# A gated feed-forward kernel behind inducing-point attention: gate and value products issued back to back, a pipelined prologue, and early output weights

## The chip, the cores and the metric

The kernel runs on one core of a Trainium2 chip. The metric is the device time of one execution in microseconds. The engines are named PE (TensorE, matmul; PEld is its weight load), DVE (VectorE), ACT (ScalarE), POOL (GpSimd) and SP (SyncE, which issues most of the DMAs). A run more than 1.5% above the fastest of the same kernel is marked slow; ratios are of fast runs alone.

## The reference, cut to what matters

Two stages run over 4 batches of 12416 tokens of 128 features: attention through 32 inducing points, then a gated feed-forward layer of width 1536 with a gated residual.

```python
h = mab(inducing, x)                 # softmax over all tokens of the batch, 32 x 128
attn = mab(x, h)                     # each token: softmax over the 32 rows of h
g   = attn @ w_gate ; val = attn @ w_val          # 128 -> 1536
ffn = (gelu(g) * val) @ w_out                     # 1536 -> 128
out = attn + sigmoid(attn @ w_res) * ffn
```

Since attn is a mix of 32 rows of h, the kernel multiplies h by the weights once per batch (the "first layers" hg, hv, hr). Each token then needs only its 32 softmax weights (rt, transposed, in four copies) against those small matrices.

## The kernel before

Tokens go in groups of 512 (100 groups, 25 per batch, of which the last is a quarter). A full group has six slots. A slot makes two chunks of 128 hidden features: a gate pair and a value pair of matmuls (two row halves of 64 side by side), a gelu on ACT and a multiply on DVE. The output products of the group before are spread between them.

```python
    def gate_slot(gi, si):
        gv_t[gi, si] = wide_bank()           # one of three double banks of PSUM
        slot_mms(gi, si, hg_t)               # gate pair into the bank
        act.activation(ge, gv_t[gi, si], AC.Gelu, ...)
    def value_mms(gi, si):
        slot_mms(gi, si, hv_t)               # value pair into the SAME bank, so after the gelu
    def value_mul(gi, si):
        ve.tensor_tensor(u, ge, gv_t.pop((gi, si)), AL.mult)
    ...
            gate_slot(*nxt)                          # the gate pair of the next slot
            if prev and p == nper - 1:
                prev.mms(len(prev.todo)); ...; prev.end()   # DVE final multiply, POOL add, store
            if prev: prev.mms(quota // 2)            # 5 output products of the group before
            value_mms(gi, p); value_mul(gi, p)
            if prev: prev.mms(quota - quota // 2)    # 5 more
            if prev and p == 0:   prev.gate()        # 4 mixing products (32 rows), ACT tanh
            elif prev and p == 2: prev.residual()    # 4 mixing products (64 rows), ACT copy
            for f in todo.pop((g, p), []): f()       # pieces of the next batch's attention
```

The prologue handles the first batch's attention tile by tile: load x, split it on DVE and POOL into a high and a low fp16 half, transpose on PE, evict on ACT, score on PE, exponential on ACT, accumulate on PE. Ahead of the loop it makes all softmax weights of tiles 0 to 7, and only then loads and scales the output weights:

```python
    for j0 in range(PRE, 8 * PRE, 4 * PRE):
        ...
        for k in range(j0 // PRE, j1 // PRE):
            weights_b(0, k)                          # POOL multiply, DMA transpose by SP
    for o in range(0, FCH, PRE):
        sy.dma_start(wf, moe_w_out ...)              # SP's queue: behind the transposes
        ve.tensor_scalar(wO[...], wf, 0.5, None, op0=AL.mult)   # DVE's queue: ahead of the multiplies
```

The softmax here doesn't subtract the row's maximum and nothing guards it: scores larger than these inputs give would overflow.

Of the kernel before, what the change touches and what calls it, by code (L numbers as in the profile page):

```python
# [9 lines left out]
FP32 = mybir.dt.float32  # L10
# [4 lines left out]
AL = mybir.AluOpType  # L15
# [3 lines left out]
def kernel(  # L19
# [24 lines left out]
    M = inducing.shape[0]  # L44
    F = moe_w_gate.shape[1]
# [34 lines left out]
    def misc_bank():  # L80
        return ps_m.tile([P, TOK], FP32, name="ms", tag="ms")
# [7 lines left out]
    def blocks_of(k):  # L89
        return k * PRE, min(PRE, nblk - k * PRE)  # L90
# [110 lines left out]
    def res_layer(b):  # L201
        bank = misc_bank()
        pe.matmul(bank[:, :P], ht_t[b], wR, start=True, stop=True)
        hr = p_h.tile([P, P], FP16, name="hr", tag="hr")
        hr_t[b] = hr
        act.activation(hr, bank[:, :P], AC.Copy, bias=0.0, scale=1.0)

    def exp_b(b, j0, j1):
        n = (j1 - j0) * M
# [69 lines left out]
    def value_mms(gi, si):  # L279
        slot_mms(gi, si, hv_t)  # L280
# [7 lines left out]
    class Last:  # L288
# [17 lines left out]
                pe.matmul(self.ffn[:, k, :], u_t[self.gi, si][:, o:o + P], wO[:, fc, :],  # L306
                          start=(fc == 0), stop=(fc == FCH - 1))

        def mix(self, h, r):
            bank = misc_bank()  # L310
            for k in range(self.nk):
                pe.matmul(bank[:, k * P:(k + 1) * P],  # L312
                          rt_t[self.b, self.k][r, self.j0 + k, :],
                          h[r, :], start=True, stop=True)
            return bank

        def gate(self):
            bank = self.mix(hr_t[self.b], slice(0, M))
            self.th = p_fin.tile([P, TOK], FP32, name="th", tag="th")
            act.activation(self.th[:, :self.tw], bank[:, :self.tw], AC.Tanh,  # L320
                           bias=0.0, scale=0.5)

        def residual(self):
            bank = self.mix(ha_t[self.b], slice(0, 2 * M))
            self.at = p_fin.tile([P, TOK], FP32, name="at", tag="at")
            act.activation(self.at[:, :self.tw], bank[:, :self.tw], AC.Copy,  # L326
                           bias=0.0, scale=1.0)
# [42 lines left out]
    pieces = []  # L370
    for dst, src in ((wG, moe_w_gate), (wV, moe_w_val), (wR, moe_w_res)):
        n = dst.shape[1]
        for o in range(0, n, PRE * P):
            w = min(PRE * P, n - o)
            pieces.append((dst[:, o:o + w], src[:, o:o + w], w))

    def weight_in(i):
        dst, src, w = pieces[i]
        wf = p_x.tile([P, PRE, P], FP32, name="xf", tag="xf")
        xf_t["w", i] = wf  # L380
        sy.dma_start(wf.rearrange("p k c -> p (k c)")[:, :w], src)

    def weight_cast(i, eng):
        dst, src, w = pieces[i]
        eng.tensor_copy(dst, xf_t.pop(("w", i)).rearrange("p k c -> p (k c)")[:, :w])


    for k in range(ntile):
        convert(0, k, ve, po if k % 2 else ve)
        if k + 3 < ntile:  # L390
            fetch(0, k + 3)
        elif k + 3 - ntile < len(pieces):
            weight_in(k + 3 - ntile)
        turn_pe(0, k)
        n0, w = blocks_of(k)
        exp_a(0, n0, n0 + w)
        if k:
            p0, pw = blocks_of(k - 1)
            accumulate(0, p0, p0 + pw, k == 1, False)
    n0, w = blocks_of(ntile - 1)  # L400
    for i in range(len(pieces)):
        weight_cast(i, po)
        if i + 3 < len(pieces):
            weight_in(i + 3)
    accumulate(0, n0, n0 + w, False, True)
    finish_h(0)
    turn_h(0)
    half = PRE // 2
    e2 = exp_b(0, 0, PRE)
    norm_b(0, 0, PRE, e2)  # L410
    weights_b(0, 0, 0, half)
    weights_b(0, 0, half, PRE)
    for i, c0 in enumerate(range(0, F, 2 * TOK)):
        c1 = min(c0 + 2 * TOK, F)
        first_layer(hg_t[0], wG, 0, c0, c1, act)
        first_layer(hv_t[0], wV, 0, c0, c1, ve)
    res_layer(0)
    for j0 in range(PRE, 8 * PRE, 4 * PRE):
        j1 = min(j0 + 4 * PRE, 8 * PRE)
        e2 = exp_b(0, j0, j1)  # L420
        norm_b(0, j0, j1, e2)
        for k in range(j0 // PRE, j1 // PRE):
            weights_b(0, k)
    for o in range(0, FCH, PRE):
        w = min(PRE, FCH - o)
        wf = p_x.tile([P, PRE, P], FP32, name="xf", tag="xf")
        sy.dma_start(wf[:, :w, :], moe_w_out.rearrange("(f p) d -> p f d", p=P)[:, o:o + w, :])
        ve.tensor_scalar(wO[:, o:o + w, :], wf[:, :w, :], 0.5, None, op0=AL.mult)
    warm = ps_f.tile([P, TOK // P, P], FP32, name="ffn", tag="ffn")
    for i in range(14):  # L430
        pe.matmul(warm.rearrange("p k c -> p (k c)"), wG[:, :P], wG[:, :TOK],
                  start=True, stop=True)

# [3 lines left out]
    def plan(b):  # L437
        todo = {}

        def at(g, p, f):  # L440
            todo.setdefault((g, p), []).append(f)

        nb = b + 1
        if nb < B:
            for k in range(ntile):
                g = k if k < 10 else k + 1
                at(g, 1, lambda k=k: fetch(nb, k))
                at(g + 1, 1, lambda k=k: convert(nb, k, po, po))
                at(g + 1, 4, lambda k=k: turn(nb, k))

        def part_two():
            for j0, j1 in ((nfull, nblk - 1), (nblk - 1, nblk)):
                norm_b(b, j0, j1, exp_b(b, j0, j1))

        def burst_one():
            part_two()
            if nb < B:
                exp_a(nb, 0, 4 * PRE)
                exp_a(nb, 4 * PRE, 8 * PRE)
        at(10, 3, burst_one)  # L460
        for i, k in enumerate(range(8, ntile)):
            at(11 + i // 2, 2 * (i % 2), lambda k=k: weights_b(b, k))
        if nb < B:
            for h in range(2):
                for i in range(2):
                    j0 = (4 * h + 2 * i) * PRE
                    at(11 + h, 3 + i, lambda j0=j0, i=i: accumulate(
                        nb, j0, j0 + 2 * PRE, i == 0, i == 1))

            def burst_two():  # L470
                exp_a(nb, nfull, nblk - 1)
                exp_a(nb, nblk - 1, nblk)
            at(16, 3, burst_two)
            at(17, 3, lambda: accumulate(nb, nfull, nfull + 2 * PRE, True, False))
            at(17, 4, lambda: accumulate(nb, nfull + 2 * PRE, nblk, False, True))
            at(18, 1, lambda: finish_h(nb))
            at(18, 3, lambda: turn_h(nb))
            spots = [(18, 4), (18, 5), (19, 1), (19, 3), (19, 4)]
            for c0 in range(0, F, 2 * TOK):
                c1 = min(c0 + 2 * TOK, F)  # L480
                at(*spots.pop(0), lambda c0=c0, c1=c1: first_layer(hg_t[nb], wG, nb, c0, c1, act))
                at(*spots.pop(0), lambda c0=c0, c1=c1: first_layer(hv_t[nb], wV, nb, c0, c1, act))
            at(*spots.pop(0), lambda: res_layer(nb))

            def burst_three():
                for j0, j1 in ((0, 4 * PRE), (4 * PRE, 8 * PRE)):
                    norm_b(nb, j0, j1, exp_b(nb, j0, j1))
            at(20, 3, burst_three)
            for i in range(8):
                at(20 + (i + 2) // 3, 2 * ((i + 2) % 3), lambda i=i: weights_b(nb, i))  # L490
        return todo
# [4 lines left out]
    for gi in range(ngrp):  # L496
        slots = groups[gi][4]
        g = gi % gpb
        nper = len(slots)
        if g == 0:  # L500
            todo = plan(groups[gi][0])
        cur = Last(gi)
        quota = -(-len(prev.todo) // (nper - 1)) if prev else 0
        for p in range(nper):
            nxt = (gi, p + 1) if p + 1 < nper else (gi + 1, 0)
            if nxt[0] < ngrp:
                gate_slot(*nxt)
            if prev and p == nper - 1:
                prev.mms(len(prev.todo))
                if nper == 2:  # L510
                    prev.residual()
                prev.end()
            if prev:
                prev.mms(quota // 2)
            value_mms(gi, p)
            value_mul(gi, p)
            if prev:
                prev.mms(quota - quota // 2)
            if prev and p == 0:
                prev.gate()  # L520
            elif prev and p == 2:
                prev.residual()
            for f in todo.pop((g, p), []):
                f()
        if g == gpb - 1:
            assert not todo, list(todo)
        prev = cur
# [34 lines left out]
```

## Time and profile before

| | before |
|---|---|
| median of 2 runs | 1056.0 us (1054.63 to 1057.37) |
| profiled execution, span | 1045.0 us |
| PE / DVE / ACT / POOL busy | 86% / 77% / 73% / 34% |
| one plain group (interval of DVE's final multiplies) | 8.95 us |
| first final multiply | 95.27 us |
| last final multiply | 1041.51 us |

The interval of the final multiplies is the most useful ruler here: there is one per group, and nothing else in the trace is so regular. Lines of the profile are given in the prediction below. In the list of costly groups, the numbers behind the first bar are the group's busy time in us and the mean length of one instruction in ns. Behind the second bar stands the idle time of the engine just before them, and what ended most of it.

### The profile page before, as it was taken

How to read it: one execution, taken by the hardware profiler on the slowest of the kernel's cores; microseconds unless marked ns; L12 is line 12 of the kernel's file. 1: busy time of each engine (PE TensorE's matmuls, PEld its weight loads, DVE VectorE, ACT ScalarE, POOL GpSimd, SP SyncE). 2: the span in 40 equal slices, each digit the busy share in tenths (PEclk: the TensorE clock that was granted, in tenths of full speed). 3: DMA queues.
4: the chain of work that ended last, by engine and by line, in shares of the span. 5: the costliest groups of instructions: out<-in, count | busy, mean ns of one | idle time of the engine just before them, and what ended most of it. 6: DMA issues, size and time to landing. Idle time of an engine off the chain costs nothing.

```text
span 1045.0 us, 23183 instructions
## 1 busy us (share of the span) xinstructions
PE 896.1 (86%) x9536; PEld 487.5 (47%) x9536; DVE 804.8 (77%) x776; ACT 768.0 (73%) x879; POOL 353.1 (34%) x308
## 2 busy tenths in 40 slices
PE   4618998999789899898889999898889899889997
PEld 3404444545445444444445444455444444444444
DVE  6317887787678888687777888678777888788886
ACT  4416788677867778778777877778777778887775
POOL 3452553621162554351134444441125111141111
PEclk9967998899989999899989999899998999999999
DMA  6362452510043444440022545340014000030000
GB/s 212 103 125 72 122 121 63 123 45 22 22 92 95 114 115 106 69 90 32 21 61 72 121 117 114 78 115 33 21 34 100 27 29 31 32 73 31 32 30 35
DMA packets 114186, 77.04 MB, mean 74 GB/s; under 512 B 92416, under 2 KB 95136, under 8 KB 114080
## 3 DMA queue, kind: packets, MB, share of 16 engines
q1 hardware_dynamic: 114080, 75.57, 28.7%
q8 instruction: 74, 1.21, 0.5%
q14 instruction: 32, 0.26, 0.1%
HBM read 27.87 MB, written 25.43 MB: 51 GB/s over the span
## 4 chain that ended last, share of the span: by engine, by line
PE 73%; DVE 11%; ACT 7%; issue 5%; DMA 2%; POOL 1%; SPq 0%; DVEq 0%; POOLq 0%; ACTq 0%
PE ffn L306 34%; PE gv L267 30%; PE ms L312 6%; DVE th L331 5%; DVE u L285 5%; ACT ge L276 2%; ACT xt L123 1%; PE gv L122 1%; PE gv L132 1%; DMA rt<-a 1%; ACT e L213 1%; DVE z L220 1%; PE ms L153 1%; ACT e L140 1%; POOL a L234 1%
## 5 line engine op out<-in xcount | busy, mean ns | idle before, releaser
L285 DVE TENSOR_TENSOR u<-ge,gv 128x1024 bf16<-128x1024 f32 x584 | 701.7, 1215 | 171.1 <-PE gv L267 167.9
L276 ACT ACTIVATE ge<-gv 128x1024 f32<-128x1024 f32 x584 | 593.0, 1019 | 112.4 <-PE gv L267 98.2
L306 PE MATMUL ffn<-wO,u 128*128 128x128 bf16 x4656 | 438.5, 226 | 21.4 <-DVE th L331 19.6
L306 PEld LDWEIGHTS <-u 128*128 128x128 bf16 x4656 | 276.9, 99 | 252.6 <-issue 241.2
L334 POOL TENSOR_TENSOR at<-at,th 128x512 f32<-128x512 f32 (+1 forms) x100 | 123.9, 1239 | 598.2 <-ACT ge L276 312.8
L267 PE MATMUL gv<-rt,hg 64*128 64x512 f16 (+1 forms) x1200 | 250.9, 392 | 84.2 <-DVE u L285 70.9
L267 PE MATMUL gv<-rt,hv 64*128 64x512 f16 (+1 forms) x1200 | 235.6, 392 | 9.1 <-ACT ge L276 9.1
L267 PEld LDWEIGHTS <-hg 64*128 64x128 bf16 x1200 | 77.6, 94 | 161.1 <-issue 124.5
L320 ACT ACTIVATE th<-ms 128x512 f32<-128x512 f32 (+1 forms) x100 | 58.5, 585 | 84.1 <-PE ms L312 81.8
L234 POOL TENSOR_TENSOR a<-e,z 128x1024 f16<-128x1024 f32 (+2 forms) x53 | 92.2, 1753 | 44.2 <-DVE z L221 32.0
L267 PEld LDWEIGHTS <-hv 64*128 64x128 bf16 x1200 | 66.2, 93 | 73.8 <-issue 20.8
L107 POOL TENSOR_TENSOR lo<-xf,hi 128x1024 f16<-128x1024 f32 (+1 forms) x45 | 90.8, 2018 | 19.4 <-DVE hi L105 19.0
L326 ACT ACTIVATE at<-ms 128x512 f32<-128x512 f32 (+1 forms) x100 | 58.4, 584 | 41.5 <-PE ms L312 41.5
L331 DVE SCALAR_TENSOR_TENSOR th<-th,ffn 128x512 f32<-128x512 f32 (+1 forms) x100 | 66.4, 664 | 6.1 <-ACT th L320 4.7
L312 PEld LDWEIGHTS <-rt 32*128 32x128 f16 (+1 forms) x776 | 44.7, 95 | 24.8 <-issue 5.6
L312 PE MATMUL ms<-ha,rt 64*128 64x128 f16 x388 | 39.3, 221 | 2.4 <-ACT th L320 2.4
L105 POOL CAST hi<-xf 128x1024 f16<-128x1024 f32 (+1 forms) x39 | 38.2, 981 | 8.4 <-DMA xf<-in_x_dram 8.4
L312 PE MATMUL ms<-hr,rt 32*128 32x128 f16 x388 | 40.0, 223 | 0.5 <-ACT at L326 0.5
L132 PEld LDWEIGHTS <-xt 128*128 128x128 f16 x776 | 22.8, 98 | 24.7 <-ACT xt L123 17.1
L132 PE MATMUL gv<-I1T,xt 128*128 128x32 f16 x388 | 13.7, 182 | 18.7 <-ACT xt L123 13.8
L220 DVE TENSOR_REDUCE z<-e 128x32 f32<-128x1024 f32 (+3 forms) x17 | 15.1, 887 | 13.8 <-ACT e L213 13.8
L123 ACT ACTIVATE xt<-gv 128x1024 f16<-128x1024 f16 (+1 forms) x13 | 12.6, 967 | 16.4 <-PE gv L122 16.4
(58 smaller groups left out, 237.2 us busy)
## 6 DMA issues: line engine op xcount, KB each, us to landing
xf<-in_x_dram SPq DMA_DIRECT2D x48, 512.0 KB, 4.2
out_dram<-at SPq DMA_DIRECT2D x96, 256.0 KB, 2.1
rt<-a SPq DMA_TRANSPOSE x53, 3.1
xt<-hi SPq DMA_TRANSPOSE x39, 4.5
xf<-in_moe_w_gate_dram SPq DMA_DIRECT2D x1, 512.0 KB, 3.4
xf<-in_moe_w_val_dram SPq DMA_DIRECT2D x1, 512.0 KB, 3.8
xf<-in_moe_w_out_dram SPq DMA_DIRECT2D x1, 512.0 KB, 4.5
xf<-in_x_dram SPq DMA_DIRECT2D x4, 64.0 KB, 2.1
```

What stands on the lines that cost most here:

```text
L107: e_lo.tensor_tensor(lo[:, :w, :P], xf[:, :w, :], hi[:, :w, :], AL.subtract)
L132: pe.matmul(bank[:, (j - j0) * M:(j - j0 + 1) * M], xt_t[b, k][:, jj, :], rows, start=True, stop=True)
L234: po.tensor_tensor(a2[:, :n], ev[:, o:o + n, :].unsqueeze(2).to_broadcast([P, n, Q, M]), z[:, 1, o:o + n].unsqueeze(2).unsqueeze(3).to_bro ...
L267: pe.matmul(v[:, c * tw:(c + 1) * tw], weights[b][r, (c0 + c) * P:(c0 + c + 1) * P], rt[r, :], start=True, stop=True)
L276: act.activation(ge[:, :n], gv_t[gi, si][:, :n], AC.Gelu, bias=0.0, scale=1.0)
L285: ve.tensor_tensor(u[:, :n], ge_t.pop((gi, si))[:, :n], gv_t.pop((gi, si))[:, :n], AL.mult)
L306: pe.matmul(self.ffn[:, k, :], u_t[self.gi, si][:, o:o + P], wO[:, fc, :], start=(fc == 0), stop=(fc == FCH - 1))
L312: pe.matmul(bank[:, k * P:(k + 1) * P], rt_t[self.b, self.k][r, self.j0 + k, :], h[r, :], start=True, stop=True)
L320: act.activation(self.th[:, :self.tw], bank[:, :self.tw], AC.Tanh, bias=0.0, scale=0.5)
L326: act.activation(self.at[:, :self.tw], bank[:, :self.tw], AC.Copy, bias=0.0, scale=1.0)
L331: ve.scalar_tensor_tensor(self.th[:, :tw], self.th[:, :tw], 1.0, self.ffn.rearrange("p k c -> p (k c)")[:, :tw], AL.add, AL.mult)
L334: po.tensor_tensor(self.at[:, :tw], self.at[:, :tw], self.th[:, :tw], AL.add)
```

## The change

The intent: PE loses time at each change between the 64-row pairs and the 128-row output products, so let gate and value pairs touch. Start faster by taking the tiles in a pipeline, and bring all weights over ACT's queue while PE and ACT are at the tiles. The diff, cut to its core:

```diff
-            if prev:
-                prev.mms(quota // 2)
             value_mms(gi, p)
+            (at the last slot: flush, residual of short groups, end)
             value_mul(gi, p)
             if prev:
-                prev.mms(quota - quota // 2)
+                prev.mms(quota)
@@ gate mix: 64 rows, the low half of hr in rows 32 to 63
+        ve.tensor_tensor(hr[M:2 * M, :], bank[M:2 * M, :P], hr[M:2 * M, :], AL.subtract)
-            bank = self.mix(hr_t[self.b], slice(0, M))
+            bank = self.mix(hr_t[self.b])            # slice(0, 2 * M) for both mixes
@@ prologue
-    for k in range(ntile):
-        convert(0, k, ve, po if k % 2 else ve)
+    for k in range(ntile + 2):
+            convert(0, k, ve, ve) ; turn_pe(0, k)    # tile k
+            weight_in(k // 2 - 1)                    # even k >= 2: act.dma_start
+            weight_cast((k - 3) // 2)                # odd k >= 3: POOL, w_out times 0.5
+            exp_a(0, n0, n0 + w)                     # tile k - 1
+            accumulate(0, ...)                       # tile k - 2
@@ loop of batch 0
+            for i in range(1, 8):
+                at((i - 1) // 2, 2 + 3 * ((i - 1) % 2), lambda i=i: weights_b(0, i))
@@ first layers of the next batch
-            spots = [(18, 4), (18, 5), (19, 1), (19, 3), (19, 4)]      # all on ACT
+            burst_three: exp_b, first_layer(hg, ve), exp_b, first_layer(hv, ve), norms
+            the narrow ones (512) on ACT at (19, 1) and (19, 4)
```

More of the change, by code (lines that the diff above doesn't have):

```diff
@@ L307, in mms, with mix @@
                           start=(fc == 0), stop=(fc == FCH - 1))
-        def mix(self, h, r):
+        def mix(self, h):
             bank = misc_bank()
+            r = slice(0, 2 * M)
             for k in range(self.nk):
@@ L323, in residual @@
         def residual(self):
-            bank = self.mix(ha_t[self.b], slice(0, 2 * M))
+            bank = self.mix(ha_t[self.b])
             self.at = p_fin.tile([P, TOK], FP32, name="at", tag="at")
@@ L372 @@
         n = dst.shape[1]
-        for o in range(0, n, PRE * P):
-            w = min(PRE * P, n - o)
-            pieces.append((dst[:, o:o + w], src[:, o:o + w], w))
-    def weight_in(i):
-        dst, src, w = pieces[i]
-        wf = p_x.tile([P, PRE, P], FP32, name="xf", tag="xf")
-        xf_t["w", i] = wf
-        sy.dma_start(wf.rearrange("p k c -> p (k c)")[:, :w], src)
-    def weight_cast(i, eng):
-        dst, src, w = pieces[i]
-        eng.tensor_copy(dst, xf_t.pop(("w", i)).rearrange("p k c -> p (k c)")[:, :w])
@@ L388 @@
-    for k in range(ntile):
-        convert(0, k, ve, po if k % 2 else ve)
-        if k + 3 < ntile:
-            fetch(0, k + 3)
-        elif k + 3 - ntile < len(pieces):
-            weight_in(k + 3 - ntile)
-        turn_pe(0, k)
-        n0, w = blocks_of(k)
-        exp_a(0, n0, n0 + w)
-        if k:
-            p0, pw = blocks_of(k - 1)
-            accumulate(0, p0, p0 + pw, k == 1, False)
-    n0, w = blocks_of(ntile - 1)
-    for i in range(len(pieces)):
-        weight_cast(i, po)
-        if i + 3 < len(pieces):
-            weight_in(i + 3)
@@ L405 @@
-    accumulate(0, n0, n0 + w, False, True)
+        for o in range(0, n, 2 * TOK):
+            w = min(2 * TOK, n - o)
+            pieces.append((dst[:, o:o + w], src[:, o:o + w], w, 1.0))
+    for o in range(0, FCH, PRE):
+        w = min(PRE, FCH - o)
+        pieces.append((wO[:, o:o + w, :].rearrange("p f d -> p (f d)"),
+                       moe_w_out.rearrange("(f p) d -> p f d", p=P)[:, o:o + w, :], w * P, 0.5))
+    staged = {}
+    def weight_in(i):
+        dst, src, w, mul = pieces[i]
+        wf = p_ge.tile([P, 2 * TOK], FP32, name="ge", tag="ge")
+        staged[i] = wf
+        v = wf[:, :w]
+        act.dma_start(v.rearrange("p (f d) -> p f d", d=P) if len(src.shape) == 3 else v, src)
@@ new lines, in weight_cast @@
+    def weight_cast(i):
+        dst, src, w, mul = pieces[i]
+        if mul == 1.0:
+            po.tensor_copy(dst, staged.pop(i)[:, :w])
+        else:
+            po.tensor_scalar(dst, staged.pop(i)[:, :w], mul, None, op0=AL.mult)
+    for k in range(ntile + 2):
+        if k < ntile:
+            convert(0, k, ve, ve)
+            if k + 3 < ntile:
+                fetch(0, k + 3)
+            turn_pe(0, k)
+        if 2 <= k and k % 2 == 0 and k // 2 - 1 < len(pieces):
+            weight_in(k // 2 - 1)
+        if 3 <= k and k % 2 and (k - 3) // 2 < len(pieces):
+            weight_cast((k - 3) // 2)
+        if 1 <= k <= ntile:
+            n0, w = blocks_of(k - 1)
+            exp_a(0, n0, n0 + w)
+        if k >= 2:
+            n0, w = blocks_of(k - 2)
+            accumulate(0, n0, n0 + w, k == 2, k == ntile + 1)
@@ L406 @@
+    weight_cast(len(pieces) - 1)
     finish_h(0)
@@ L408 @@
     half = PRE // 2
-    e2 = exp_b(0, 0, PRE)
-    norm_b(0, 0, PRE, e2)
+    norm_b(0, 0, PRE, exp_b(0, 0, PRE))
     weights_b(0, 0, 0, half)
     weights_b(0, 0, half, PRE)
+    more = [exp_b(0, j0, min(j0 + 4 * PRE, 8 * PRE)) for j0 in (PRE,)]
     for i, c0 in enumerate(range(0, F, 2 * TOK)):
@@ L417 @@
     res_layer(0)
-    for j0 in range(PRE, 8 * PRE, 4 * PRE):
-        j1 = min(j0 + 4 * PRE, 8 * PRE)
-        e2 = exp_b(0, j0, j1)
-        norm_b(0, j0, j1, e2)
-        for k in range(j0 // PRE, j1 // PRE):
-            weights_b(0, k)
-    for o in range(0, FCH, PRE):
-        w = min(PRE, FCH - o)
-        wf = p_x.tile([P, PRE, P], FP32, name="xf", tag="xf")
-        sy.dma_start(wf[:, :w, :], moe_w_out.rearrange("(f p) d -> p f d", p=P)[:, o:o + w, :])
-        ve.tensor_scalar(wO[:, o:o + w, :], wf[:, :w, :], 0.5, None, op0=AL.mult)
+    more.append(exp_b(0, 5 * PRE, 8 * PRE))
+    norm_b(0, PRE, 5 * PRE, more[0])
+    norm_b(0, 5 * PRE, 8 * PRE, more[1])
     warm = ps_f.tile([P, TOK // P, P], FP32, name="ffn", tag="ffn")
-    for i in range(14):
+    for i in range(10):
         pe.matmul(warm.rearrange("p k c -> p (k c)"), wG[:, :P], wG[:, :TOK],
@@ L443, in plan @@
         nb = b + 1
+        if b == 0:
+            for i in range(1, 8):
+                at((i - 1) // 2, 2 + 3 * ((i - 1) % 2), lambda i=i: weights_b(0, i))
         if nb < B:
@@ L477, in plan @@
             at(18, 3, lambda: turn_h(nb))
-            spots = [(18, 4), (18, 5), (19, 1), (19, 3), (19, 4)]
-            for c0 in range(0, F, 2 * TOK):
-                c1 = min(c0 + 2 * TOK, F)
-                at(*spots.pop(0), lambda c0=c0, c1=c1: first_layer(hg_t[nb], wG, nb, c0, c1, act))
-                at(*spots.pop(0), lambda c0=c0, c1=c1: first_layer(hv_t[nb], wV, nb, c0, c1, act))
-            at(*spots.pop(0), lambda: res_layer(nb))
-            def burst_three():
-                for j0, j1 in ((0, 4 * PRE), (4 * PRE, 8 * PRE)):
-                    norm_b(nb, j0, j1, exp_b(nb, j0, j1))
+            cs = [(c0, min(c0 + 2 * TOK, F)) for c0 in range(0, F, 2 * TOK)]
+            def burst_three():
+                e0 = exp_b(nb, 0, 4 * PRE)
+                first_layer(hg_t[nb], wG, nb, *cs[0], ve)
+                e1 = exp_b(nb, 4 * PRE, 8 * PRE)
+                first_layer(hv_t[nb], wV, nb, *cs[0], ve)
+                norm_b(nb, 0, 4 * PRE, e0)
+                norm_b(nb, 4 * PRE, 8 * PRE, e1)
             at(20, 3, burst_three)
+            at(19, 1, lambda: first_layer(hg_t[nb], wG, nb, *cs[1], act))
+            at(19, 4, lambda: first_layer(hv_t[nb], wV, nb, *cs[1], act))
+            at(19, 3, lambda: res_layer(nb))
             for i in range(8):
@@ L507 @@
                 gate_slot(*nxt)
+            value_mms(gi, p)
             if prev and p == nper - 1:
@@ L512 @@
                 prev.end()
-            if prev:
-                prev.mms(quota // 2)
-            value_mms(gi, p)
             value_mul(gi, p)
             if prev:
-                prev.mms(quota - quota // 2)
+                prev.mms(quota)
             if prev and p == 0:
```

## The prediction

> **What bounds the kernel now.** I read the summary page first (engine shares, chain of waits, costliest groups), then the instructions in order of time in one steady stretch, then the first 100 us, and last the busy times in 7 us stretches, for the clock. From the page, the chain that ended last and the four costliest groups:
>
> ```profile
> PE 73%; DVE 11%; ACT 7%; issue 5%; DMA 2%; POOL 1%; SPq 0%; DVEq 0%; POOLq 0%; ACTq 0%
> ...
> L285 DVE TENSOR_TENSOR u<-ge,gv 128x1024 bf16<-128x1024 f32 x584 | 701.7, 1215 | 171.1 <-PE gv L267 167.9
> L276 ACT ACTIVATE ge<-gv 128x1024 f32<-128x1024 f32 x584 | 593.0, 1019 | 112.4 <-PE gv L267 98.2
> L306 PE MATMUL ffn<-wO,u 128*128 128x128 bf16 x4656 | 438.5, 226 | 21.4 <-DVE th L331 19.6
> ...
> L267 PE MATMUL gv<-rt,hg 64*128 64x512 f16 (+1 forms) x1200 | 250.9, 392 | 84.2 <-DVE u L285 70.9
> ```
>
> PE carries 73% of the chain, and both DVE and ACT wait for PE's gate and value products (167.9 and 98.2 us). So PE bounds the steady state, but DVE (77% busy) and ACT (73%) are close behind. Next, the steady stretch in order of time (start, duration, engine, line, operation, count, and the idle time before it):
>
> ```profile
> 308.34 0.10 PEld L267 LDWEIGHTS <-hg 64*128 64x128 bf16 x2
> 308.35 0.39 PE L267 MATMUL gv<-rt,hg 64*128 64x512 f16 x2
> 308.66 0.28 PEld L306 LDWEIGHTS <-u 128*128 128x128 bf16 x5 [0.23 <-issue]
> 308.67 0.45 PE L306 MATMUL ffn<-wO,u 128*128 128x128 bf16 x5
> ...
> 309.05 0.39 PE L267 MATMUL gv<-rt,hv 64*128 64x512 f16 x2
> ...
> 309.65 0.39 PE L267 MATMUL gv<-rt,hg 64*128 64x512 f16 x2
> ...
> 309.88 0.38 PE L267 MATMUL gv<-rt,hv 64*128 64x512 f16 x2
> ...
> 310.83 0.39 PE L267 MATMUL gv<-rt,hg 64*128 64x512 f16 x2 [0.57 <-DVE u L285]
> ```
>
> Gate pair to the output products behind it: 308.67-308.35 = 0.32 us. Five output products to the next pair: 0.38. But where two pairs touch (309.65, 309.88) it is 0.23. Five output products span 0.45 with the last one 0.226, so they issue every 0.056 us and fill only 0.28 of the 0.38. Each change between pair and output block thus costs about 0.10, the length of one weight load (0.10 in the rows). A slot is now gate, 5, value, 5: 2x0.32 + 2x0.38 = 1.40 us with four changes. At the end of a group PE also waits 0.57 for a buffer (last row). The final multiply (L331) recurs every 8.95 us in 63 of the 99 steps: that is one group of 512 tokens. The third thing is the start:
>
> ```profile
> 69.10 1.90 POOL L234 TENSOR_TENSOR a<-e,z 128x1024 f16<-128x1024 f32 x1 [1.35 <-DMA rt<-a]
> 72.31 1.25 SPq L427 DMA_DIRECT2D xf<-in_moe_w_out_dram  x2
> ...
> 76.83 1.25 DVE L428 TENSOR_SCALAR wO<-xf 128x1024 bf16<-128x1024 f32 x2 [22.15 <-DMA xf<-in_moe_w_out_dram]
> 77.99 7.34 DVE L285 TENSOR_TENSOR u<-ge,gv 128x1024 bf16<-128x1024 f32 x6
> 79.26 0.61 PE L267 MATMUL gv<-rt,hg 64*128 64x512 f16 x2 [22.05 <-DVE u L285]
> ```
>
> The output weights are requested at 72.31, since their issue stands in the sync engine's queue behind nine transposes that wait for POOL. DVE stands 22.15 us before their conversion, PE behind DVE. The stretches of 7 us show a granted clock of 0.50 from about 60 to 90 us and for some 10 us after two of the three bursts of exponentials of each batch.
>
> **What the Trainium skill says.** "TensorE: Matmul & The Clock Gate", part 3, What overlaps and what doesn't: a weight load runs ahead of a matmul in flight only when the row groups differ (part 2 adds the background weight buffer). The trace agrees in part: loads hide within a block and between pairs, and one of 0.10 us shows at every change between 64-row and 128-row products. The same page, Architectural detail: ACT and DVE queues are strict first in, first out; the 22.15 us show it. Its part 1: PE's clock is halved after an idle window of some 3.4 us; here the lowest granted clock is 0.50. "Trainium Kernel Development and Optimization", Key Constraints: DMAs issued by different engines share the 16 DMA engines, and only issue time is saved. So the ACT queue brings the weights no bandwidth, only freedom from the wait above.
>
> **The change, part by part.**
>
> *Slots.* The order becomes gate(s+1), value(s), 10 output products: 0.23 + 0.32 + (10x0.056 + 0.10) = 1.21 us, two changes instead of four, 0.19 less. The mixing products cost 0.33 extra for the gate (32 rows; 303.55 to 303.88) and 0.22 for the residual (64 rows; 0.54 where a pair alone is 0.32); both now use 64 rows, so 0.11 less. PE per group: 12x0.225 + five blocks x0.20 + 48x0.056 + 2x0.22 = 6.8 us, where before 7.9 and about 1.0 of waits made 8.95.
>
> PE then no longer sets the period alone. A gelu starts 0.44 after its gate pair (305.29 to 305.73), lasts 1.02, and the value pair, which overwrites the same bank, starts 0.06 after its end (55.84 to 55.90). So value follows its own gate by at least 1.52. Before, 5 output products stood between; now the reach is one slot plus 0.23. I follow a group by hand, V0 = 0 being the value pair of slot 0, with ACT taking 0.92 per gelu back to back (1.94 us for two) and 0.50 per tanh or copy: mix at 0.98, tanh 1.41, gate(2) 1.20, gelu(2) 1.91 to 2.93, V2 = 2.99 instead of 2.64. V3 = 4.42; the copy at 4.40 delays gelu(4) to 4.90, so V4 = 5.98 instead of 5.63; eight products, gate of the next slot 0 at 6.85, V5 = 7.08. Its gelu runs 7.29 to 8.31, so the next V0 = 8.37. DVE keeps up: six multiplies at 1.12 to 1.22 and a final one at 0.60 make 7.3 to 8.0. The period is **8.37**, a saving of 0.58 of 8.95, not the 1.1 that PE sheds.
>
> 63 steps x0.58 = 37; 28 steps with bursts or half clock x0.5 (an estimate: their exponentials and table loads are unchanged) = 14; the shorter batch ends 3. Sum **54 us**.
>
> *First layers in bursts.* Two 1024-wide ones per batch go from ACT to DVE, inside a burst in which DVE waits anyway. The steps around the old places exceed 8.95 by 0.64 and 4.03; I take 2 of that back, three times, less some DVE time: **5 us**.
>
> *Prologue.* A tile takes 3.04 us now (transposes at 14.08, 17.12, 20.16), a chain PE, ACT, PE, ACT. Pipelined, it is bound by DVE (0.73 + 1.14 = 1.87 for both conversions, POOL's 2.12 going to DVE), PE (about 1.95) or the loads (three buffers: (1.87+4.2)/3 = 2.0). With weights competing I take 2.2 to 2.3. The sum at 43.03 then comes near 35: 8 us. From there to the first gate pair it is 11.4 now; four warm-up products fewer make about 10.5.
>
> *Output weights.* Loaded early, they take the 22 us wait away. Group 0 then runs at about 1.3 us a slot from 47; its final multiply follows one group later, near 64 with some 2 us for a cold clock, against 95.27 now. Prologue and output weights together: **31 us**.
>
> Sum: 54 + 5 + 31 = 90. On the measured 1056: **966 us**; I say 965.
>
> **Rivals.** (1) PE's 1.1 us per group are realized in full. It needs ACT to have slack; by the 1.52 us above it has none. With 0.5 us more over some 95 groups it would give some 918. (2) The new wait for gelu, or DVE at 8.0, eats the steady gain wholly: 8.9 per group, 1015 in all. For it: DVE is 77% busy before. Against: the multiplies drop to 1.12 when queued. (3) POOL becomes late: seven softmax weight products (1.9) move into groups 0 to 3, where with two conversions (1.04+2.13) and the final add (1.27) they make about 8.2 of 8.4. Outputs have a group of slack, so 0 to 10 us. (4) The loads bind the prologue: 9 MB at the 230 GB/s seen there would be 39 us, and its 8 us vanish. (5) The clock falls in the emptier PE stream. A stretch with PE 4.43 of 7.00 us busy kept 1.00 before, so I don't expect it.
>
> **Range and chances.** The prologue is 31 within 8; the steady part 54 within 20 (0.2 us per group is 20). Combined: 940 to 995. Even rival 2 stays below 1035, so faster 0.97, same 0.02, slower 0.01.
>
> **What would show it.** Right: the final multiplies recur every 8.2 to 8.5 us; value pairs wait on ACT three times a group; the wait for gate and value products before DVE's multiply shrinks; no wait of 22 us; the first final multiply at 60 to 70 us. Wrong: a period above 8.7 or below 8.0, DVE's multiplies all back to back, or half clock in plain groups.

## The result

| | before | changed | predicted |
|---|---|---|---|
| median of 2 runs | 1056.0 us | 960.15 us (958.98 to 961.32) | 965 |
| ratio of fast runs | | 0.909, 95% interval 0.902 to 0.916 | |
| span of the profiled execution | 1045.0 | 959.5 | |
| plain group | 8.95 | 8.41 | 8.37 |
| first final multiply | 95.27 | 68.91 | near 64 |
| last minus first final multiply | 946.24 | 886.74 | 59 less |

A ratio is the mean time of one kernel's fast runs over the mean of the other's fast runs of the same rounds, so it is not quite the ratio of the medians in the tables. Ratios of different rounds should not be compared to the last digit: the kernel before took 1056 in this one, and 1046 to 1050 in the rounds of the experiments. Against those, 960.15 would be some 0.917 (an estimate from the medians).

The 85.5 us between the spans are made up of 26.4 at the start and 59.5 between the first and last final multiply, less 0.4 at the tail. The page of the changed kernel, the chain by engine and the costliest groups:

```profile
PE 11%; ACT 9%; DVE 6%; issue 3%; ACTq 0%; DVEq 0%; POOLq 0%
...
L286 DVE TENSOR_TENSOR u<-ge,gv 128x1024 bf16<-128x1024 f32 x584 | 693.9, 1214 | 103.4 <-PE gv L268 100.7
L277 ACT ACTIVATE ge<-gv 128x1024 f32<-128x1024 f32 x584 | 571.3, 1020 | 61.0 <-PE gv L268 59.1
L307 PE MATMUL ffn<-wO,u 128*128 128x128 bf16 x4656 | 353.1, 224 | 0.2
...
L268 PE MATMUL gv<-rt,hv 64*128 64x512 f16 (+1 forms) x1200 | 257.3, 385 | 65.8 <-ACT ge L277 64.8
```

The chain is followed back only over the last 29% of the span here, but within it PE no longer has three quarters: PE 11, ACT 9 and DVE 6 share it, which fits a ring of engines that wait for each other. The groups say the same. DVE's and ACT's waits for PE have fallen (167.9 to 100.7 and 98.2 to 59.1 us), and a wait has appeared that hardly existed before: PE's value pairs wait 64.8 us for ACT's gelu. The output products' busy time has fallen from 438.5 to 353.1 us for the same 4656 instructions: a block of ten spans 0.73, where two blocks of five spanned 0.45 each.

A plain group in order of time (start, duration, engine, line, operation, count, idle before):

```profile
111.04 0.39 PE L268 MATMUL gv<-rt,hg 64*128 64x512 f16 x2 [0.29 <-DVE u L286]
111.65 0.39 PE L268 MATMUL gv<-rt,hv 64*128 64x512 f16 x2 [0.22 <-ACT ge L277]
111.97 0.73 PE L307 MATMUL ffn<-wO,u 128*128 128x128 bf16 x10
...
113.13 0.60 ACT L322 ACTIVATE th<-ms 128x512 f32<-128x512 f32 x1 [0.62 <-PE ms L314]
113.62 1.94 ACT L277 ACTIVATE ge<-gv 128x1024 f32<-128x1024 f32 x2
...
114.06 0.39 PE L268 MATMUL gv<-rt,hg 64*128 64x512 f16 x2
114.69 0.39 PE L268 MATMUL gv<-rt,hv 64*128 64x512 f16 x2 [0.24 <-ACT ge L277]
115.02 0.73 PE L307 MATMUL ffn<-wO,u 128*128 128x128 bf16 x10
...
117.67 0.39 PE L268 MATMUL gv<-rt,hv 64*128 64x512 f16 x2 [0.18 <-ACT ge L277]
```

A value pair that need not wait would start 0.23 us behind the gate pair. In slot 2 it starts 0.63 behind (114.06 to 114.69): the tanh at 113.13 pushed gelu(2) to 113.62, and the value pair waits for that gelu's end. The copy does the same to slot 4 (117.67), and slot 0 waits for its own gelu (111.65). These are the three waits that the prediction names.

The start of the changed kernel:

```profile
29.15 1.37 DVE L105 CAST hi<-xf 128x1024 f16<-128x1024 f32 x1 [3.37 <-DMA xf<-in_x_dram]
...
39.08 0.43 DVE L160 COPY nacc<-ms 128x257 f32<-128x257 f32 x1 [2.09 <-PE ms L155]
...
41.68 4.24 POOL L396 TENSOR_SCALAR wO<-ge 128x1024 bf16<-128x1024 f32 x2 [5.07 <-DMA ge<-in_moe_w_out_dram]
...
46.74 2.04 POOL L235 TENSOR_TENSOR a<-e,z 128x512 f16<-128x512 f32 x2
...
51.23 0.61 PE L268 MATMUL gv<-rt,hg 64*128 64x512 f16 x4 [1.31 <-DMA rt<-a]
```

The 22 us wait is gone. But the sum over the tiles (L160) comes at 39.08, not near 35: DVE waited for x, 3.37 us at one tile. And the first gate pair follows 12.15 us later, not 10.5: POOL's conversion of the output weights takes 4.24 us and stands ahead of the first softmax weights (46.74), whose transposes PE awaits.

One more thing stands in this stretch. In the kernel before, the granted clock was 1.00 up to about 55 us; here it was 0.50 from 30 to 45 us and again from 55 to 60. The stretch of 25 to 30 us, with the 3.37 us wait for x, had PE busy for 0.74 us only. The clock did not decide the second delay, though: pe_more below, with the same prologue, kept 1.00 up to 50 us and took 12.49 from sum to gate pair.

### The profile page after: what moved, and what is told of

The parts are those of the page before. It is cut to its first block, busy times and chain, and to the rows that moved or that the text cites. A ratio compares the mean times of both kernels' runs of the same rounds, so it can differ in the third digit from the quotient of the medians.

```text
span 959.5 us, 23172 instructions
## 1 busy us (share of the span) xinstructions
PE 811.1 (85%) x9532; PEld 470.6 (49%) x9532; DVE 808.0 (84%) x790; ACT 738.5 (77%) x873; POOL 344.9 (36%) x304
## 5 line engine op out<-in xcount | busy, mean ns | idle before, releaser
L286 DVE TENSOR_TENSOR u<-ge,gv 128x1024 bf16<-128x1024 f32 x584 | 693.9, 1214 | 103.4 <-PE gv L268 100.7
L277 ACT ACTIVATE ge<-gv 128x1024 f32<-128x1024 f32 x584 | 571.3, 1020 | 61.0 <-PE gv L268 59.1
L307 PE MATMUL ffn<-wO,u 128*128 128x128 bf16 x4656 | 353.1, 224 | 0.2
L268 PE MATMUL gv<-rt,hv 64*128 64x512 f16 (+1 forms) x1200 | 257.3, 385 | 65.8 <-ACT ge L277 64.8
L268 PE MATMUL gv<-rt,hg 64*128 64x512 f16 (+1 forms) x1200 | 259.5, 389 | 46.0 <-DVE u L286 33.1
L268 PEld LDWEIGHTS <-hv 64*128 64x128 bf16 x1200 | 103.1, 95 | 148.8 <-issue 146.7
L107 POOL TENSOR_TENSOR lo<-xf,hi 128x1024 f16<-128x1024 f32 (+1 forms) x39 | 78.1, 2002 | 0.4
L314 PEld LDWEIGHTS <-rt 64*128 64x128 f16 x776 | 44.4, 95 | 23.5 <-issue 4.1
L314 PE MATMUL ms<-hr,rt 64*128 64x128 f16 x388 | 40.1, 225 | 0.7 <-ACT at L328 0.7
L122 PE MATMUL gv<-identF,hi 128*128 128x128 f16 x97 | 11.9, 295 | 15.0 <-DVE hi L105 14.9
```

The lines of the kernel that those rows point to most:

```text
L107: e_lo.tensor_tensor(lo[:, :w, :P], xf[:, :w, :], hi[:, :w, :], AL.subtract)
L268: pe.matmul(v[:, c * tw:(c + 1) * tw], weights[b][r, (c0 + c) * P:(c0 + c + 1) * P], rt[r, :], start=True, stop=True)
L277: act.activation(ge[:, :n], gv_t[gi, si][:, :n], AC.Gelu, bias=0.0, scale=1.0)
L286: ve.tensor_tensor(u[:, :n], ge_t.pop((gi, si))[:, :n], gv_t.pop((gi, si))[:, :n], AL.mult)
L307: pe.matmul(self.ffn[:, k, :], u_t[self.gi, si][:, o:o + P], wO[:, fc, :], start=(fc == 0), stop=(fc == FCH - 1))
L314: pe.matmul(bank[:, k * P:(k + 1) * P], rt_t[self.b, self.k][r, self.j0 + k, :], h[r, :], start=True, stop=True)
```

## The experiments

Theory G: after the change, PE waits in each plain group for the gelu of the slot, because the value pair follows its gate pair too closely; that, not PE's own work, sets 8.41. The rivals: PE still binds (P), or DVE does (D), or most of the gain is the start (S). "First final" below is the start of the first final multiply, "period" the interval in plain groups, both from the traces. All outputs are right. Each set of rounds also ran the kernel before; its medians there were 1046 to 1050 us. The expectations for the parts were reckoned from 1056, so some 6 to 10 us of their totals lie in the base; ratio, period and first final are the safer readings.

### The parts alone

**slot_only**: the kernel before with the new order of a slot.

```diff
-            if prev: prev.mms(quota // 2)
             value_mms(gi, p)
+            (flush and end at the last slot)
             value_mul(gi, p)
-            if prev: prev.mms(quota - quota // 2)
+            if prev: prev.mms(quota)
```

> The kernel before with the new slot order alone (gate pair, value pair, ten output products). Theory G (value pairs now wait for their own gelu, 1.52 us behind their gate pair): plain groups fall from 8.95 to about 8.4 us, because the gate's 32-row mix delays nothing but PE; total about 1003 us, 998 to 1012. Rival P (PE alone sets the period, so the two changes saved per slot are realized in full, 1.0 us a group): about 960. Rival S (most of the gain is the start): 1035 or more.

Measured: 984.3 us, ratio 0.940 (0.936 to 0.945), period 8.41 as in the whole change, first final 93.54. The total is better than expected, and lies between the 1003 of Theory G and the 960 of Rival P. The period decides between them: 8.41 is Theory G's, Rival P's full 1.0 us a group would have made about 7.95. Of the surplus of 19 us some 6 are the base. Most of the rest is in the steps behind the bursts: those after the first burst of the first three batches took 10.17 us each where the kernel before took 13.19 to 13.46, at a granted clock of 0.99 to 1.00 instead of 0.69 to 0.70. Rivals P and S are both out: the reordering alone brings about two thirds of the gain.

**start_only**: the changed kernel with the old slot order, old gate mix and old places of the first layers.

```diff
+            (the loop, the 32-row mix and the spots of the kernel before)
```

> The changed kernel with the old slot order, the old 32-row gate mix and the old places of the first layers: only the start differs from before (pipelined tiles, all weights over ACT's queue, softmax weights of tiles 1 to 7 inside the loop). First final multiply near 70 us instead of 95.27, so about 26 us less: 1030, 1025 to 1036. A rival in which POOL's moved work makes the first groups late: 1040 or more.

Measured: 1023.9 us, ratio 0.978 (0.972 to 0.984), first final 70.24, period 8.95. First final and period are as expected; the total lies just under the range, which was reckoned from 1056.

**wout_early**: the kernel before, only the output weights moved.

```diff
+        act.dma_start(wf, moe_w_out ...)              # at tiles 2 and 4
+        po.tensor_scalar(wO ..., wf, 0.5, None, op0=AL.mult)   # at tiles 4 and 6
-        sy.dma_start(wf ..., moe_w_out ...) ; ve.tensor_scalar(wO ..., wf ...)
```

> The kernel before with only the output weights changed: loaded over ACT's queue during the first tiles and converted on POOL there. Theory W (of the start's 26 us, the 22 us wait is nearly all): no wait of 22 us, first final multiply near 73 us instead of 95.27, total some 22 us less, ratio 0.975 to 0.985. Rival T (the pipelined tiles and the moved softmax weights carry most of it): less than 12 us, ratio above 0.989.

Measured: 1032.6 us, ratio 0.985 (0.976 to 0.994), first final 71.93. The times alone do not separate the two theories, the interval is too wide; the trace does:

```profile
54.36 0.61 PE L267 MATMUL gv<-rt,hg 64*128 64x512 f16 x4
...
56.37 7.21 DVE L285 TENSOR_TENSOR u<-ge,gv 128x1024 bf16<-128x1024 f32 x6 [1.73 <-PE gv L267]
```

The first gate pair stands where it stood before (54.39), and DVE's multiplies begin at 56.37 instead of 77.99. The first final comes 23.3 us earlier, against 25.0 for the whole start in start_only. So pipelining the tiles and moving seven softmax products into the loop brought only about 2 us there, net of the delay on POOL shown above.

**gate64_only**: the kernel before with the 64-row gate mix.

```diff
+        ve.tensor_tensor(hr[M:2 * M, :], bank[M:2 * M, :P], hr[M:2 * M, :], AL.subtract)
-            bank = self.mix(hr_t[self.b], slice(0, M))
+            bank = self.mix(hr_t[self.b], slice(0, 2 * M))
```

> The kernel before with only the 64-row gate mix (low half of the gate matrix in rows 32 to 63). Before is bound by PE, and the trace puts the 32-row mix at 0.33 and the 64-row one at 0.22: 0.11 x some 92 groups = 10 us less, 1046, period 8.84. If the wait at the end of the group takes it back: 1056.

Measured: 1034.1 us, ratio 0.987 (0.982 to 0.992), period 8.85. So 0.10 us of PE per group is worth 0.10 us of time while PE binds. In the changed kernel the same saving is worth nothing: slot_only has the old 32-row mix and the same period, 8.41.

**layers_only**: the kernel before with the first layers moved into the third burst.

```diff
-            spots = [(18, 4), (18, 5), (19, 1), (19, 3), (19, 4)]   # first layers on ACT
+            e0 = exp_b(...); first_layer(hg, ve); e1 = exp_b(...); first_layer(hv, ve)
```

> The kernel before with only the first layers of the next batch moved into the third burst. From the two traces the four steps concerned shrink by some 4.8 us a batch, of which 2.3 is the shorter period, so about 2.5 x 3 = 7 us: 1049. If their cost was only moved from one step to another: 1056.

Measured: 1048.4 us, ratio 1.001 (0.996 to 1.007). The expectation from the two traces was wrong, although 1049 seems to be met: it was 1056 less 7, and the kernel before took 1049.7 in these rounds. In batch 0 the two steps concerned, 12.98 and 13.35 us before, became 9.98 and 16.53: the cost moved with the work, 26.33 against 26.51 in sum. As a check of the parts: slot_only's 984.3 less the 24.6 us by which the changed kernel's first final lies ahead of slot_only's is 959.7; the changed kernel took 960.15. Nothing clear of the spread is left for the gate mix and the first layers.

### What sets 8.41

**pe_more**: eight useless mixing products more per group, at the ends of slots 1 and 3.

```diff
+            elif prev and p in (1, 3) and nper > 2:
+                prev.mix(ha_t[prev.b])
```

> The changed kernel with eight useless 64-row mixing products more per group (four at the end of slot 1, four at the end of slot 3; nobody reads them), about 0.44 us of PE. Theory G: they fall into PE's waits for gelu ahead of the value pairs of slots 2 and 4 (0.35 to 0.40 us each), period stays 8.41 to 8.5, total 960 to 968. Rival P (PE binds): 0.44 x 94 = 41 us more, about 1001.

Measured: 966.5 us, period 8.41, unchanged to the hundredth. The additional work went into PE's waits, as the wait of the value pairs shows (for what, total us, times, longest):

```profile
PE gv L268 <- ACT ge L277: 35.3, 102, 1.1
```

It was 64.8 in 241 waits. Rival P is out for the changed kernel. The 6 us more of total time lie in the burst groups, which are not plain.

**act_more**: the tanh of each group done twice.

```diff
+            for _ in range(2):
                 act.activation(self.th ..., AC.Tanh, ...)
```

> The changed kernel with the tanh of a group done twice (same result), 0.50 us of ACT more per group in slot 0. Theory G: gelu(2) starts 0.5 later, the value pair of slot 2 with it, and nothing takes it back: period 8.9, total about 1007 (1000 to 1012). Rivals P (PE binds) and D (DVE binds, at 8.0 of 8.41): under 970.

Measured: 1015.5 us, over the expected range; period 9.04, 0.63 more.

```profile
114.37 1.23 ACT L323 ACTIVATE th<-ms 128x512 f32<-128x512 f32 x2 [0.62 <-PE ms L314]
115.30 0.39 PE L268 MATMUL gv<-rt,hg 64*128 64x512 f16 x2
115.49 1.94 ACT L277 ACTIVATE ge<-gv 128x1024 f32<-128x1024 f32 x2
...
116.56 0.39 PE L268 MATMUL gv<-rt,hv 64*128 64x512 f16 x2 [0.87 <-ACT ge L277]
```

The second tanh, which overwrites the result of the first, costs 0.63 instead of the 0.50 of an independent one. PE's wait before the value pair of slot 2 grows from 0.24 to 0.87, and the whole 0.63 arrives in the period. So ACT's work in that place lies on the ring, while PE's at the ends of slots 1 and 3 does not. DVE, with the same work, had slack. Rival D is out for the changed kernel.

**mix_ahead**: the mixing products ahead of the output products of their slot.

```diff
             value_mul(gi, p)
+            if prev and p == 0: prev.gate()
+            elif prev and p == 2: prev.residual()
             if prev:
                 prev.mms(quota)
-            if prev and p == 0: prev.gate()
-            elif prev and p == 2: prev.residual()
```

> The changed kernel with the mixing products of a group moved ahead of the ten output products of their slot, so that tanh and copy reach ACT 0.66 us earlier, before the next gate pair is done, and no longer delay a gelu. Theory G: the waits of slots 2 and 4 shrink from 0.4 to about 0.1, the one of slot 0 stays: period 7.85, total about 910 (900 to 925). Rival D (DVE at 8.0 unless its multiplies run back to back): 922 or more. Rival P: 960.

Measured: 909.6 us, ratio 0.868 (0.863 to 0.872), period 7.78.

```profile
113.71 0.39 PE L268 MATMUL gv<-rt,hv 64*128 64x512 f16 x2 [0.22 <-ACT ge L277]
113.92 0.38 PE L314 MATMUL ms<-hr,rt 64*128 64x128 f16 x4
114.24 0.73 PE L307 MATMUL ffn<-wO,u 128*128 128x128 bf16 x10
114.46 0.60 ACT L322 ACTIVATE th<-ms 128x512 f32<-128x512 f32 x1
...
116.10 0.39 PE L268 MATMUL gv<-rt,hg 64*128 64x512 f16 x2
...
116.41 0.39 PE L268 MATMUL gv<-rt,hv 64*128 64x512 f16 x2
```

Not one instruction has been removed. The tanh now runs before the next gelu is due, and the value pair of slot 2 (116.41) stands 0.31 behind its gate pair instead of 0.63. The wait of slot 0 is still there. Over the whole span PE's waits for gelu fall from 241 to 97, about one a group. It is the strongest evidence for Theory G, since the edit moves nothing but the mixing products and, with them, ACT's two small instructions.

**mix_between**: the mixing products between gate and value pair.

```diff
             gate_slot(*nxt)
+            if prev and p == 0: prev.gate()
+            elif prev and p == 2: prev.residual()
             value_mms(gi, p)
@@ behind the output products
-            (the same four lines)
```

> As mix_ahead, but the mixing products stand between the gate pair and the value pair, where PE waits for gelu anyway. Theory G: period 7.55 to 7.7 with DVE about to bind, total 885 to 900. Rival D: as mix_ahead, no better than 915.

Measured: 893.6 us, ratio 0.852 (0.848 to 0.857), period 7.64.

```profile
112.85 0.68 DVE L333 SCALAR_TENSOR_TENSOR th<-th,ffn 128x512 f32<-128x512 f32 x1
...
113.44 7.12 DVE L286 TENSOR_TENSOR u<-ge,gv 128x1024 bf16<-128x1024 f32 x6
120.48 0.68 DVE L333 SCALAR_TENSOR_TENSOR th<-th,ffn 128x512 f32<-128x512 f32 x1
```

The mixing products fill PE's wait in slot 0. DVE now does one final multiply and six multiplies without a gap: from 113.44 for 7.12 us, to 120.56, just past 120.48, where the next final multiply begins. So DVE is busy for 7.57 of the 7.63 us of a plain group and leaves no room for a shorter period. PE is close behind: it was busy for 7.38, and the chain of the page gives PE 59% and DVE 27%. That work taken off DVE alone would shorten the period further was not tested.

### The start

**pool_order**: POOL converts the output weights behind the first softmax weights.

```diff
-    weight_cast(len(pieces) - 1)            # and the one before, inside the tiles
     finish_h(0)
     ...
     weights_b(0, 0, half, PRE)
+    for i in range(5, len(pieces)):
+        weight_cast(i)
```

> The changed kernel with POOL's two conversions of the output weights behind the first softmax weights instead of ahead of them. If the start lost time to their 4.24 us on POOL, the sum stays at 39.1, the softmax weights start near 44.3 instead of 46.74 and the first gate pair near 49 instead of 51.23; total about 2 us less (956 to 960). If the chain does not run there: first gate pair at 51.

Measured: 957.8 us, ratio 0.913 (0.908 to 0.919), first gate pair 48.17, first final 66.48. The sum came at 38.09, 1 us earlier than in the changed kernel, and the gate pair 10.08 us behind it instead of 12.15, so 2 us of the start were POOL's. The runs bear it out: the six with POOL's old order took 11.4 to 12.5 from sum to gate pair (the changed kernel, start_only, pe_more, act_more, mix_ahead, mix_between), the three with the new order 10.1 to 10.8. The 1 us at the sum is not the edit's: it varies between runs with the same tile code (see below). In total time the 2 us are within the noise of these rounds.

**loads_late**: besides, no weights requested before the tenth tile.

```diff
-        if 2 <= k and k % 2 == 0 and k // 2 - 1 < len(pieces):
-            weight_in(k // 2 - 1)
+        if k in (9, 10, 11):
+            weight_in(k - 9)
+        if k in (12, 13):
+            weight_cast(k - 12); weight_in(k - 9)
+    (the output weights requested behind the sum)
```

> As pool_order, and the weights are requested only when ten tiles of x are on their way (nothing of them competes with x before). If the loads bind the pipelined tiles, as rival 4 of the prediction has it, DVE's waits for x of 2.16 and 3.37 us vanish and the sum comes to 32 to 34 us instead of 39.08; the first layers may then wait for their weights, so first gate pair 44 to 48, total 952 to 957. If the tiles are bound by PE, DVE and the pipeline itself: sum at 37 or later.

Measured: 952.9 us, ratio 0.909 (0.903 to 0.914), first gate pair 44.20, first final 61.65.

```profile
33.42 0.43 DVE L160 COPY nacc<-ms 128x257 f32<-128x257 f32 x1 [1.87 <-PE ms L155]
```

The sum comes 5.7 us earlier than in the changed kernel with the same tile pipeline, and DVE's waits for x fall from 8.2 to 3.6 us. Five other runs with the changed kernel's prologue had the sum at 36.4 to 38.1 and waited 5.3 to 7.0 for x, so 3 to 5.7 us is the fair size; best_b repeats it with 33.92. So the loads bound the tiles there: x and weights shared the DMA engines, and requesting the weights over another queue did not change that.

**best_b**: mix_between and loads_late together.

```diff
+            (both edits above)
```

> mix_between and loads_late together. They act on different stretches (the period of a group; the start), so their gains should add: 893.6 less the 7 us that loads_late took from the changed kernel, about 887 (883 to 891), first final multiply near 60 us, period 7.64. If the earlier start is eaten by POOL or by a cold clock in the first groups: 891 or more.

Measured: 889.4 us (887.4 to 894.3, six runs), ratio 0.848 (0.844 to 0.853) to the kernel before, period 7.64, first final 61.17. The gain over mix_between in the medians is 4 us, less than the 7 expected; the first final is 5.9 us earlier, the rest is within the spread of the runs. It is the fastest kernel here, though not clearly apart from mix_between.

## Why the prediction was right

**The slot.** Right, and by its own step: the value pair's reach of 1.52 us behind the gate pair. The recurrence gave a period of 8.37 where 8.41 was measured, with waits in the slots it named, and mix_ahead removed two of them. The rival that PE's saving is realized in full (918) falls with the period of slot_only and with pe_more. The rival that the new wait eats everything (1015) falls with the period.

**Steps that are not plain.** The 63 steps counted as plain gave 32.1 us (37 predicted). Only 58 of them stand within 0.03 us of 8.95, and one of these, behind the last burst, fell into half clock in the changed kernel (9.88 us at a clock of 0.73). The other 36 steps gave 27.4 of the 59.5 us, where 14 + 3 + 5 = 22 were predicted. That the sum is right to 0.5 us is therefore luck: one term was too large, another too small, and one was nothing:

**First layers.** "5 us" was wrong: the term measures nothing (layers_only, 1.001). I had taken the excess of a step as the cost of the work placed there; it moved with the work into the burst. In its place in the sum stand above all the steps behind the bursts, which the estimate of 0.5 us a step did not model: that after the first burst fell from 13.22 to 11.30 us at a clock of 0.69 and 0.85, that after the third from 12.49 to 9.41 at 0.62 and 0.82. This half-clock time varies within one run: behind the second burst the changed kernel took 11.72, 9.92 and 11.51 us in three batches, at clocks of 0.71, 0.90 and 0.72.

**Prologue.** "8 us" at the sum was mis-sized: it measured 4.0 (43.03 to 39.08), and 5.0 to 6.6 in the five other runs with this prologue. The rival that the loads bind was the truth, as loads_late shows; that the sum stood at its very 39 is partly chance. I had taken 2.2 to 2.3 us a tile from the engines' side. The step from sum to first gate pair, predicted to shrink to 10.5, grew to 12.15. I had counted POOL's conversion among the hidden work without asking what stands behind it in POOL's queue; pool_order gives 10.08, close to the 10.5 predicted.

**Output weights.** Right: the wait of 22 us vanished, and wout_early alone moved the first final by 23.3 us. Start in all: 26.4 of the 31 predicted. The first final came 4.9 us behind the 64 predicted: the two points above lost 4.1 and 1.7, and the first group gave 0.8 back.

**POOL late in the first groups.** Predicted as 0 to 10 us, seen as none: the first plain steps of the changed kernel are 8.35 and 8.41 from the first one on.

**The clock.** No half clock in plain groups, as expected, but for the step behind the last burst. The half clock from 30 to 45 us, among the tiles, was not foreseen; the prediction had a cold clock only for the first group.

In total the steady part came 0.5 us better and the start 4.6 us worse than predicted; the time came 5 us lower than the figure given, because the profiled execution of before, from which the parts were reckoned, was 9 us faster than the 1056 from which they were taken. So the closeness of 965 to 960 is luck in part; the period is not.

## What to carry to other kernels

When an edit takes work off the bounding engine, write down who must finish before each of its instructions and how long that takes from its own release; the longest such chain around a slot or a group is the new bound, and here it ate half of what PE had shed. Then look for small instructions of another engine that stand in that reach: moving the products of a tanh and a copy ahead of an output block took 0.63 us off the period, where the reordering had taken 0.54, and removed nothing. An excess found in one stretch of a trace is not yet the cost of the work that stands there, and a fast new queue brings no bandwidth.

## What the Trainium skill lacked or had wrong

- "TensorE: Matmul & The Clock Gate", part 3, What overlaps and what doesn't, gives the rule for when a weight load is hidden. No page that I read, the note on mode switching in "TensorEngine Tiling (Array Packing)" included, gives a time for changing between row-tiled and full-array products. Here a change costs about 0.10 us: pair to pair 0.23, pair to output block 0.32, and a block of ten 0.66 for 0.56 of issue.
- "TensorE: Matmul & The Clock Gate", part 1, says that the ramp penalty, that of the warm-up, is under 1% of a typical span. It gives no figure for how much half clock that comes back later spreads the times of one program. Here the kernel before took 1042.5 to 1057.5 us over the eleven runs beside best_b, 1.4%, in step with mean granted clocks of 0.954 to 0.935. In which steps those runs differed was not traced.
- "Perfetto Trace Analysis", Optimizing Scalar/DVE Operations, says that the write-acknowledgement half of an instruction's access overhead overlaps with the next instruction. The traces agree in kind: a gelu of 1.02 us repeats every 0.92, and a tanh or copy of 0.60 holds back the next gelu by 0.50. What the page does not say is what becomes of it when the next instruction writes the same tile: the second tanh costs 0.63, so nothing overlaps there.
- No page that I read gives a difference between POOL's copy and its multiply by a constant. Converting 1024 and 512 columns from fp32 to bf16 as a copy took 1.04 us and 0.61 to 0.95 us on POOL in the changed kernel; with the multiply by 0.5 it took 2.77 and 1.49.
